# Convolution, token mix and channel mix on one Trainium2 core: five edits to the order of copies, block transfers and last sums

## The chip, the cores and the metric

The kernel runs on one core of one Trainium2 chip. What counts is the device time of one execution in microseconds, and the number given for a kernel is the median of its runs. The kernel before took 2002.95 us (median of 3 runs, 2002.93 to 2003.98). Of one further execution there is a hardware profile: that execution took 2004.08 us, and its span, from the first to the last recorded instruction, is 2002.3 us.

The engines are PE (TensorE, matrix products; PEld is its loading of weights), DVE (VectorE), ACT (ScalarE), POOL (GpSimd) and SP (SyncE, which here only issues transfers). PSUM is the memory into which PE sums, in banks of 512 f32 values per partition.

## The reference

```python
B, S, D = 8, 4096, 192        # batches, tokens, channels; 8 heads of 24 channels, 7 taps
w = softmax(weight)                                        # per head
x = einsum('hk,bskhg->bshg', w, windows(pad_left(x, 6)))   # causal convolution over the tokens
h = relu(x^T @ w_tok1) @ w_tok2                            # token mix, 4096 -> 256 -> 4096
u = x + h^T
out = u + relu(u @ w_ch1) @ w_ch2                          # channel mix, 192 -> 1536 -> 192
```

All is f32. PE gets each f32 operand as two parts, hi (rounded to the type fp32r) and lo (what is left), and a product is made of hi·hi, hi·lo and lo·hi.

## The kernel before, in words

**Groups and tiles.** The batches are worked in five groups: one batch, one batch, and three pairs (`GROUPS = [[0],[1],[2,3],[4,5],[6,7]]`). The tokens of a batch are cut into 8 tiles of 512 tokens. For each tile of a batch the foreground does this, one after the other:

1. Second token product ("mix2", L991/L992 for one batch, L994 to L996 and L1033 for pairs), added on DVE to the convolved input (L1003, L1004): this gives u.
2. u is turned so that channels lie on partitions. In group 0's first tile PE does it (`transposed`, L1059 to L1074). Elsewhere DVE transposes 32x32 blocks (L1006, L1018), and `blocks_sent` (L1099) brings the blocks to their partitions with 16 transfers per call, four steps `k` of four quarters `q`. A quarter with odd `q` goes out on POOL, one with even `q` on SP: 8 and 8.
3. u is split in hi and lo. For a single batch (`parted_single`) that is L1109 on ACT and L1113 on DVE. For a pair (`parted`), three chunks `c`: ACT writes the hi part (L1128, 128x512), DVE the lo part (L1130). Then the halves of the partitions are swapped for the second batch: two copies of all three chunks on ACT, hi first, then lo (L1133, 64x1536 each), and two transfers on POOL the other way (L1135).
4. Product 1 (`channel1`, L1185): six steps of 18 pairs of matmuls over 64 rows, which run on both halves of PE at once. Each step writes a pair of PSUM banks; ACT takes the hi part of relu twice (L1255, `hh`), DVE the lo part once (L1256, `hl`). A step of two sums needs a free pair of banks, so it waits for the L1256 of an earlier step.
5. Product 2 (`channel2`, L1292/L1293, or `channel2_halves`, L1274, in which both halves of PE work again), whose sums DVE adds to u (L1299 and L1303, or L1280 and L1282); then the result is stored (L1322).

PSUM has three pairs of banks for all of this (`ps_x`; `banks()` takes a pair, `bank()` the first bank of one) and two banks for the first token product (`ps_a`).

**Background.** Other work runs between the steps: the convolution of a later group (ACT L725, DVE L727, stored by POOL L762), splitting it (ACT L814, DVE L818), splitting `w_tok1` (ACT L798, DVE L802, POOL L804), the first token product of a later group ("mix1", L830, or L834 to L836 with two batches), and during group 0 also the decoding of `w_tok2` from its bits (ACT L202, L217; DVE L204, L218, L205, L208, L211) and its copying out in another order (`store_t2`: two ACT copies of 128x512, L1423, steps 0 and 1, then a transfer issued by ACT, L1425, step 2).

This is set in order by a planner in the program (`Background`), as the program is written out, not on the chip. Work stands in streams of items. The planner keeps a clock of PE (`pe`) and one of DVE (`dve`), and `fg(pe, dve)` is called at marked places of the foreground with the work of the stretch just written. `fill` then takes items while the DVE clock is less than a margin ahead of PE's: an item is ready if its gate is open and, with a `lag`, if PE's clock has run that far past the end of the item before it in the stream. Of the ready ones the stream that is least done comes first. In product 1 and `channel2_halves` PE works in halves, `bg.tiled` is set, and items that contain PE work are passed over:

```python
if self.tiled and it.pe:
    continue
```

A decoding job has the steps begin, four DVE steps, high (`high(i)`, the ACT copy L217 with lag 0) and low (L218). Jobs for the third and fourth quarter of `w_tok2` wait by their gate until the stores of an earlier quarter are done (`("stored", q2 - 2)`), and the last item of the stream of stores (`through`) opens the memory for the convolution of group 2.

**The end.** The last tokens of the kernel go through `channel2_last`: 12 matmuls hi·(hi, lo) into `both` (L1310), 12 lo·hi into `one` (L1312), the two banks of one pair; then three DVE sums, L1313 from `both`, and L1315 twice, from `both` and from `one`.

Of the kernel before, what the change touches and what calls it, by code (L numbers as in the profile page):

```python
# [22 lines left out]
class Item:  # L23
# [3 lines left out]

    def __init__(self, fn, cost=0.0, lag=0.0, pe=0.0, gate=None, tag=None, eager=False):  # L30
        self.fn, self.cost, self.lag, self.pe, self.gate, self.tag = fn, cost, lag, pe, gate, tag
        self.eager = eager


class Background:
# [52 lines left out]
    def fill(self, until):  # L88
        for s in self.streams:
            while s["items"] and s["items"][0].eager and self.may(s):  # L90
                self.pop(s)
        while True:
            ready = []
            for s in self.streams:
                if s["items"]:
                    it = s["items"][0]
                    at = it.gate() if it.gate else 0.0
                    if self.tiled and it.pe:
                        continue
                    if at is not None and (not it.lag or self.pe >= max(s["free"], at) + it.lag):  # L100
                        ready.append(s)
            if self.dve >= self.pe + until:
                ready = [s for s in ready if s["items"][0].pe]
            if not ready:
                return
            self.pop(min(ready, key=lambda s: s["done"] / s["total"] - s["lead"]))
# [33 lines left out]
def conv_mixer_kernel(ctx: ExitStack, tc: tile.TileContext, x, weight, w_tok1, w_tok2, w_ch1, w_ch2, out):  # L140
# [165 lines left out]
    def decode_items(dec, jobs, loaded=False, pause=None):  # L306
# [26 lines left out]
        def high(i):  # L333
            if not jobs[i][4]:
                return

            def fn():
                jb = sts[i]["jb"]
                hi, lo = jb["make"]() if "make" in jb else (jb["hi"], jb["lo"])
                sts[i]["b"] = dec.b(sts[i], hi, lo, jb.get("view", lambda v: v))  # L340

            add(0, 0, fn, gate=jobs[i][3])

        def low(i):
            def post():
# [737 lines left out]
    def blocks_sent(z, nb, pool, name):  # L1083

        if nb == 1:
            other = own_tile("lo")
            home = other
        else:  # L1090
            other = pool.tile([P, 2, ND, TT], F32R, name=name)
            home = other[:, 1]
        blocks = z[:, :nb * D // QB].rearrange("p (q c) t -> p q (c t)", c=ND)
        home = home.rearrange("p c t -> p (c t)").rearrange("p (i n) -> p i n", i=NQ)
        for k in range(NQ):
            for q in range(NQ):
                i = (q + k) % NQ
                queue = nc.gpsimd if q % 2 else nc.sync
                queue.dma_start(  # L1099
                    out=f32(home[q * QB:(q + 1) * QB, i]),  # L1100
                    in_=blocks[i * QB:(i + 1) * QB, q % (2 * nb)],
                )
        return other
# [16 lines left out]
    def parted(other):  # L1120


        own = own_tile("hi"), own_tile("lo")
        low, high = slice(0, D2), slice(D2, P)
        for c in range(ND):
            v = f32(by_blocks_of(other[:, 1])[:, :, c]).rearrange("p i (j e) -> p j i e", e=QB)
            hi, lo = (o[:, c].rearrange("p (j i e) -> p j i e", i=NQ, e=QB) for o in own)
            nc.scalar.copy(out=hi, in_=v)  # L1128
            bg.fg(0, 700, 0)
            nc.vector.tensor_tensor(out=lo, in0=v, in1=f32(hi), op=ALU.subtract)  # L1130
        swapped = other[:, 0], other[:, 1]
        for k in range(2):
            nc.scalar.copy(out=swapped[k][high], in_=f32(own[k][low]))  # L1133
        for k in range(2):
            nc.gpsimd.dma_start(out=f32(swapped[k][low]), in_=f32(own[k][high]))  # L1135
        own, swapped = (*own, range(ND)), (*swapped, range(ND))
        return [(own, swapped), (swapped, own)]
# [166 lines left out]

    def channel2_last(i, h, u, osb, j):
        ts = slice(j * P, (j + 1) * P)
        pair = banks()
        both, one = pair[:, 0], pair[:, 1]
        for n, f in enumerate(order):
            nc.tensor.matmul(out=both[:, :2 * D], lhsT=h["hh", f][:, ts], rhs=w2[:, f, :], start=n == 0, stop=n == NF - 1)  # L1310
        for n, f in enumerate(order):
            nc.tensor.matmul(out=one[:, :D], lhsT=h["hl", f][:, ts], rhs=w2[:, f, :D], start=n == 0, stop=n == NF - 1)  # L1312
        nc.vector.tensor_tensor(out=rows(osb[:, j]), in0=rows(both[:, :D]), in1=tokens(u, i)[:, j], op=ALU.add)  # L1313
        for v in (both[:, D:2 * D], one[:, :D]):
            nc.vector.tensor_tensor(out=osb[:, j], in0=v, in1=osb[:, j], op=ALU.add)  # L1315
# [51 lines left out]
    def first_items():  # L1367
# [14 lines left out]
        for q2 in range(NS):  # L1382
            for kc in range(KC):
                for r in range(2):
                    a = (q2, kc, r)
                    stores.append(Item(lambda a=a: store_t2(*a, 0), lag=1000, gate=staged(q2)))
                    stores.append(Item(lambda a=a: store_t2(*a, 1), lag=600))
                    stores.append(Item(lambda a=a: store_t2(*a, 2), lag=1200))
            stores.append(Item(lambda q2=q2: stored(q2)))
            for a0 in range(0, ST, TT) if q2 else []:  # L1390
# [187 lines left out]
```

## Time and profile before

| what | value |
|---|---|
| median of 3 runs | 2002.95 us (2002.93 to 2003.98) |
| profiled execution | 2004.08 us |
| its span | 2002.3 us |
| PE busy | 1993.8 us |
| DVE busy | 1465.1 us |
| ACT busy | 763.4 us |
| POOL busy | 229.9 us |

The page gives busy times of each engine, then the span in 40 slices of 50 us, each digit the busy share in tenths. The view of waits lists, for an engine, what it stood still for, in microseconds in all, how often, and the longest. The timeline lists instructions in order of their start, with start and duration in us, the line, the operation, the tiles, a count where equal ones follow one another, and in brackets the idle time before and what ended it. An arrow `a<-b` reads "a from b".

Between the profiled execution and its span lie 1.8 us.

### The profile page before, as it was taken

The numbers are of one execution on the slowest core, as the hardware profiler recorded it, in microseconds if no ns is written. First come the engines' busy times: TensorE is split into PE (matmuls) and PEld (weight loads), VectorE is DVE, ScalarE is ACT, GpSimd is POOL, SyncE is SP. The second block draws the span as 40 slices with busy tenths as digits, with TensorE's granted clock in tenths as the row PEclk, the third lists the DMA queues.
The fourth block names the chain that finished last, engine by engine and source line by source line (L and its number), as shares of the span: only waits on it lengthen the run. The fifth ranks groups of instructions, "written<-read, shape, count | busy, mean of one in ns | idle before, by whom it ended". The sixth has DMA issues, their size and how long they took to land.

```text
span 2002.3 us, 44236 instructions
## 1 busy us (share of the span) xinstructions
PE 1993.8 (100%) x18596; PEld 1846.3 (92%) x18596; DVE 1465.1 (73%) x2474; ACT 763.4 (38%) x1271; POOL 229.9 (11%) x434
## 2 busy tenths in 40 slices
PE   9999999999999999999999999999999999999999
PEld 9898999999999999999989999999999999999998
DVE  8889989999759998744797788446566656665564
ACT  5786433434343343432433433323333322333322
POOL 0001112121211101110011110111111101011110
PEclk9999999999999999999999999999999999999999
DMA  9956456575474456532466434433313233233310
GB/s 308 319 172 211 138 167 198 167 234 173 155 184 131 137 166 196 140 86 53 126 172 203 119 107 140 134 88 85 83 51 78 76 80 81 66 86 85 85 49 17
DMA packets 277046, 267.69 MB, mean 134 GB/s; under 512 B 190928, under 2 KB 224256, under 8 KB 276848
## 3 DMA queue, kind: packets, MB, share of 16 engines
q1 hardware_dynamic: 251744, 182.39, 32.3%
q0 software_dynamic: 22800, 74.08, 12.5%
q10 hardware_dynamic: 2304, 8.39, 1.1%
q8 instruction: 147, 2.41, 0.5%
q14 instruction: 51, 0.42, 0.1%
HBM read 146.31 MB, written 71.30 MB: 109 GB/s over the span
## 4 chain that ended last, share of the span: by engine, by line
PE 93%; DVE 3%; ACT 1%; DMA 1%; issue 1%; SPq 1%; ACTq 0%; DVEq 0%
PE ps_x L1185 38%; PE ps_x L1274 23%; PE ps_x L1292 11%; PE ps_x L1293 5%; PE ps_x L1033 2%; PE ps_a L834 2%; PE ps_a L835 2%; PE ps_a L836 2%; DVE xc L727 1%; PE ps_x L991 1%; PE ps_a L484 1%; PE ps_x L994 1%; PE ps_x L1222 1%; PE ps_a L830 1%; PE ps_x L996 1%; PE ps_x L995 1%
## 5 line engine op out<-in xcount | busy, mean ns | idle before, releaser
L1255 ACT ACTIVATE hh<-ps_x 128x512 fp32r<-128x512 f32 x744 | 404.5, 596 | 843.5 <-PE ps_x L1185 843.3
L1256 DVE SCALAR_TENSOR_TENSOR hl<-ps_x,hh 128x1024 fp32r<-128x1024 f32 x372 | 453.8, 1222 | 228.3 <-ACT hh L1255 227.7
L1274 PE MATMUL ps_x<-w,hh 64*128 64x384 f32 x3360 | 481.6, 355 | 0.0
L1274 PE MATMUL ps_x<-w,hl 64*128 64x192 f32 x3360 | 424.5, 247 | 0.0
L727 DVE SCALAR_TENSOR_TENSOR xc<-raw,cw,xc 128x384 f32<-128x384 f32 (+1 forms) x768 | 385.9, 560 | 7.3 <-ACT xc L725 7.3
L1292 PE MATMUL ps_x<-w,hh 128*128 128x384 f32 x1284 | 370.1, 360 | 0.3 <-DVE hl L1256 0.3
L1185 PE MATMUL ps_x<-other,w_hi 64*128 64x512 f32 x1296 | 336.9, 388 | 0.7 <-ACT other L1133 0.4
L1185 PE MATMUL ps_x<-own_hi,w_hi 64*128 64x512 f32 x1440 | 330.7, 393 | 0.5 <-DVE hl L1256 0.2
L1274 PEld LDWEIGHTS ps_x<-w,hl 64*128 64x128 f32 x3360 | 325.8, 188 | 0.9
L1185 PE MATMUL ps_x<-own_lo,w_hi 64*128 64x512 f32 x1440 | 325.4, 388 | 0.0
L1185 PE MATMUL ps_x<-own_hi,w_lo 64*128 64x512 f32 x1440 | 325.1, 387 | 0.0
L1293 PE MATMUL ps_x<-w,hl 128*128 128x192 f32 x1284 | 321.5, 250 | 0.0
L1274 PEld LDWEIGHTS ps_x<-w,hh 64*128 64x128 f32 x3360 | 319.9, 184 | 0.9
L1185 PEld LDWEIGHTS ps_x<-other,w_hi 64*128 64x128 f32 x1296 | 235.7, 184 | 23.8 <-DVE hl L1256 1.0
L1293 PEld LDWEIGHTS ps_x<-w,hl 128*128 128x128 f32 x1284 | 245.1, 191 | 0.0
L1292 PEld LDWEIGHTS ps_x<-w,hh 128*128 128x128 f32 x1284 | 241.0, 188 | 1.6 <-DVE hl L1256 1.2
L1185 PEld LDWEIGHTS ps_x<-own_lo,w_hi 64*128 64x128 f32 x1440 | 215.4, 184 | 26.0 <-ACT own_lo L1074 0.4
L1185 PEld LDWEIGHTS ps_x<-own_hi,w_lo 64*128 64x128 f32 x1440 | 215.2, 184 | 25.9
L1185 PEld LDWEIGHTS ps_x<-own_hi,w_hi 64*128 64x128 f32 x1440 | 209.5, 184 | 30.9 <-issue 4.1
L1185 PE MATMUL ps_x<-other,w_lo 64*128 64x512 f32 x648 | 181.5, 386 | 0.0
L1282 DVE TENSOR_TENSOR osb<-ps_x,osb 128x192 f32<-128x192 f32 x420 | 150.0, 357 | 14.5
L1280 DVE TENSOR_TENSOR osb<-ps_x,u 128x192 f32<-128x192 f32 x140 | 49.7, 355 | 135.5 <-PE ps_x L1274 135.5
(185 smaller groups left out, 2397.2 us busy)
## 6 DMA issues: line engine op xcount, KB each, us to landing
raw<-in_x_dram SPq DMA_DIRECT2D x56, 672.0 KB, 7.3
t<-t2d SPq DMA_DIRECT2D x64, 512.0 KB, 5.6
u<-xcd SPq DMA_DIRECT2D x62, 384.0 KB, 7.4
xcd<-xc POOLq DMA_DIRECT2D x28, 768.0 KB, 8.4
t<-t1p SPq DMA_DIRECT2D x32, 512.0 KB, 4.3
out_dram<-osb SPq DMA_DIRECT2D x36, 384.0 KB, 3.8
out_dram<-osb POOLq DMA_DIRECT2D x27, 384.0 KB, 3.0
t2d<-stage ACTq DMA_DIRECT2D x16, 512.0 KB, 3.5
```

Source lines behind the costliest of these rows:

```text
L727: nc.vector.scalar_tensor_tensor(out=dst, in0=src, scalar=cw[:, h, k:k + 1], in1=dst, op0=ALU.mult, op1=ALU.add)
L834: nc.tensor.matmul(out=ps, lhsT=wh, rhs=xh, start=a, stop=False)
L835: nc.tensor.matmul(out=ps, lhsT=wh, rhs=xl, start=False, stop=False)
L836: nc.tensor.matmul(out=ps, lhsT=wl, rhs=xh, start=False, stop=z)
L1185: nc.tensor.matmul(out=pss[:, h], lhsT=w1[w][rows, t[h][2][c], p * P:(p + 1) * P], rhs=t[h][v][rows, c], start=a and n == 0, stop=z and n ...
L1255: nc.scalar.activation(out=hh[:, k], in_=pss[:, k], func=AF.Relu)
L1256: nc.vector.scalar_tensor_tensor(out=hl, in0=pss, scalar=0.0, in1=f32(hh), op0=ALU.max, op1=ALU.subtract)
L1274: nc.tensor.matmul(out=ps[:, :m], lhsT=h[part, f][ks, ts], rhs=w2[ks, f, :m], start=n == 0 and part == "hh", stop=z and part == "hl",)
L1280: nc.vector.tensor_tensor(out=rows(osb[:, j]), in0=rows(pss[0][:, :D]), in1=tokens(u, i)[:, j], op=ALU.add)
L1282: nc.vector.tensor_tensor(out=osb[:, j], in0=v, in1=osb[:, j], op=ALU.add)
L1292: nc.tensor.matmul(out=ps[:, :2 * D], lhsT=h["hh", f][:, ts], rhs=w2[:, f, :], start=n == 0, stop=False)
L1293: nc.tensor.matmul(out=ps[:, :D], lhsT=h["hl", f][:, ts], rhs=w2[:, f, :D], start=False, stop=z)
```

## The change

Five edits.

1. An item of the planner can be `long`. While PE works in halves, long items are passed over as those with PE work are. The two ACT copies of `store_t2` are long.
2. The high step of a decoding job has a lag of 300 instead of 0.
3. In `blocks_sent`, the transfer of the last step `k` and the quarter `q` = 0 goes out on POOL. POOL then has 9 of the 16 of a call, SP 7. There are 36 calls.
4. In `parted`, the swapped hi part is copied chunk by chunk in the loop (64x512, right behind the split of that chunk), and the swapped lo part by one copy of 64x1536 after the loop, as before. It is 48 ACT instructions more, two for each of 24 calls.
5. In `channel2_last`, `both` and `one` are the first banks of two pairs, and no longer the two banks of one pair.

```diff
@@ Item
-    def __init__(self, fn, cost=0.0, lag=0.0, pe=0.0, gate=None, tag=None, eager=False):
+    def __init__(self, fn, cost=0.0, lag=0.0, pe=0.0, gate=None, tag=None, eager=False, long=False):
         self.fn, self.cost, self.lag, self.pe, self.gate, self.tag = fn, cost, lag, pe, gate, tag
-        self.eager = eager
+        self.eager, self.long = eager, long
@@ Background.fill
-                    if self.tiled and it.pe:
+                    if self.tiled and (it.pe or it.long):
                         continue
@@ high(i), decoding
-            add(0, 0, fn, gate=jobs[i][3])
+            add(0, 300, fn, gate=jobs[i][3])
@@ blocks_sent
-                queue = nc.gpsimd if q % 2 else nc.sync
+                queue = nc.gpsimd if q % 2 or (k, q) == (NQ - 1, 0) else nc.sync
@@ parted
             nc.vector.tensor_tensor(out=lo, in0=v, in1=f32(hi), op=ALU.subtract)
+            nc.scalar.copy(out=other[high, 0, c], in_=f32(own[0][low, c]))
         swapped = other[:, 0], other[:, 1]
-        for k in range(2):
-            nc.scalar.copy(out=swapped[k][high], in_=f32(own[k][low]))
+        nc.scalar.copy(out=swapped[1][high], in_=f32(own[1][low]))
@@ channel2_last
-        pair = banks()
-        both, one = pair[:, 0], pair[:, 1]
+        both, one = bank(), bank()
@@ first_items
-                    stores.append(Item(lambda a=a: store_t2(*a, 0), lag=1000, gate=staged(q2)))
-                    stores.append(Item(lambda a=a: store_t2(*a, 1), lag=600))
+                    stores.append(Item(lambda a=a: store_t2(*a, 0), lag=1000, gate=staged(q2), long=True))
+                    stores.append(Item(lambda a=a: store_t2(*a, 1), lag=600, long=True))
```

The changed kernel has the same matmuls and the same DVE work. Line numbers are the same up to L1130; the chunk's copy is the new L1131, the lo copy stays L1133, and behind `channel2_last` lines are one less (L1310, L1312, L1313 and L1315 become L1309, L1311, L1312 and L1314; L1423 becomes L1422).

Since the planner places all of the background from its clocks, the edits 1 and 2 move it in groups 0 and 1. Three places follow, each with the program order of one engine.

**Group 0, first tile, DVE up to the first lo part of product 1** (L1256). L278 splits a weight, L1230 adds the sums of the very first tokens, L727 is the convolution, and L204 to L218 decode `w_tok2`. Before:

```order
L278 TENSOR_TENSOR w_1133<-w2f,w_1133 128x4x192 x3
L1230 TENSOR_TENSOR osb<-ps_x,u 128x192
L727 SCALAR_TENSOR_TENSOR xc_926<-raw_751,cw,xc_926 128x8x24 x2
L727 SCALAR_TENSOR_TENSOR xc_926<-raw_754,cw,xc_926 128x8x24 x6
L1230 TENSOR_TENSOR osb<-ps_x,u 128x192
L727 SCALAR_TENSOR_TENSOR xc_926<-raw_754,cw,xc_926 128x8x24 x6
L1256 SCALAR_TENSOR_TENSOR hl_1194<-ps_x,hh_1193 128x1024
```

After:

```order
L278 TENSOR_TENSOR w_1126<-w2f,w_1126 128x4x192 x3
L1230 TENSOR_TENSOR osb<-ps_x,u 128x192
L204 TENSOR_SCALAR dec_top<-dec_top 128x512
L218 TENSOR_TENSOR t2s<-dec_top,t2s 128x512
L205 TENSOR_SCALAR dec_top<-dec_top 128x512
L208 SCALAR_TENSOR_TENSOR dec_top<-dec_raw,dec_top 128x512
L211 SCALAR_TENSOR_TENSOR dec_top<-dec_raw,dec_top 128x512
L727 SCALAR_TENSOR_TENSOR xc_947<-raw_754,cw,xc_947 128x8x24 x2
L1230 TENSOR_TENSOR osb<-ps_x,u 128x192
L727 SCALAR_TENSOR_TENSOR xc_947<-raw_754,cw,xc_947 128x8x24 x6
L1256 SCALAR_TENSOR_TENSOR hl_1186<-ps_x,hh_1185 128x1024
```

Between L278 and the first L1256 stood 14 instructions of the convolution; now 8 of them and a run of five decoding steps stand there. The five stood ahead of these rows before, and six of the convolution have taken their place.

**The boundary from group 1 to group 2, DVE in product 2 of group 1's last tile.** `xc` is group 2's convolved input, L818 makes its lo part for mix1, L802 the lo part of `w_tok1`, L1113 splits u of the last tile, and L1299 and L1303 are product 2's sums of two token blocks each. Before:

```order
L1006 STREAM_TRANSPOSE own_hi<-u 128x3x2x32 x2
L802 TENSOR_TENSOR t_5468<-t_5468 128x2x256
L1299 TENSOR_TENSOR osb<-ps_x,u 128x384
L1303 TENSOR_TENSOR osb<-ps_x,osb 128x384
L818 TENSOR_TENSOR xhl<-xc_5175,xhl 128x768
L1113 TENSOR_TENSOR own_lo<-own_lo,own_hi 128x4x128 x3
L802 TENSOR_TENSOR other<-other 128x2x256
L1299 TENSOR_TENSOR osb<-ps_x,u 128x384
L1303 TENSOR_TENSOR osb<-ps_x,osb 128x384
L818 TENSOR_TENSOR xhl<-xc_5175,xhl 128x768
```

After:

```order
L1006 STREAM_TRANSPOSE own_hi<-u 128x3x2x32 x2
L727 SCALAR_TENSOR_TENSOR xc_5284<-raw_5244,cw,xc_5284 128x16x24 x2
L802 TENSOR_TENSOR t_5558<-t_5558 128x2x256
L727 SCALAR_TENSOR_TENSOR xc_5284<-raw_5244,cw,xc_5284 128x16x24 x4
L1299 TENSOR_TENSOR osb<-ps_x,u 128x384
L1303 TENSOR_TENSOR osb<-ps_x,osb 128x384
L727 SCALAR_TENSOR_TENSOR xc_5284<-raw_5244,cw,xc_5284 128x16x24 x2
L1113 TENSOR_TENSOR own_lo<-own_lo,own_hi 128x4x128 x3
L1299 TENSOR_TENSOR osb<-ps_x,u 128x384
L1303 TENSOR_TENSOR osb<-ps_x,osb 128x384
L818 TENSOR_TENSOR xhl<-xc_5284,xhl 128x768
L802 TENSOR_TENSOR other<-other 128x2x256
```

The end of the convolution came before these rows and now lies among them, and the first L818 stood ahead of L1113 and now stands behind the second L1303. The first matmul of mix1 stands at the same place in PE's order in both.

**Group 2, first tile, ACT in `parted`.** Before:

```order
L1255 ACTIVATE hh_6068<-ps_x 128x512 x4
L1128 CAST own_hi<-other 128x512 x3
L1133 CAST other<-own_hi 64x1536
L1133 CAST other<-own_lo 64x1536
L1255 ACTIVATE hh_6386<-ps_x 128x512 x4
```

After:

```order
L1255 ACTIVATE hh_6068<-ps_x 128x512 x4
L1128 CAST own_hi<-other 128x512
L1131 CAST other<-own_hi 64x512
L1128 CAST own_hi<-other 128x512
L1131 CAST other<-own_hi 64x512
L1128 CAST own_hi<-other 128x512
L1131 CAST other<-own_hi 64x512
L1133 CAST other<-own_lo 64x1536
L1255 ACTIVATE hh_6388<-ps_x 128x512 x4
```

One copy of three chunks became three of one chunk between the splits; the lo copy stayed the last.

## The prediction

> **What bounds the kernel now.** I read the page's head and its chain first, then what PE waited for, then the timeline around each wait.
>
> ```profile
> PE 1993.8 (100%) x18596; PEld 1846.3 (92%) x18596; DVE 1465.1 (73%) x2474; ACT 763.4 (38%) x1271; POOL 229.9 (11%) x434
> ...
> PE 93%; DVE 3%; ACT 1%; DMA 1%; issue 1%; SPq 1%; ACTq 0%; DVEq 0%
> ```
>
> PE is busy for 1993.8 of 2002.3 us. The change removes no matmul, so all that it can touch is what PE stands still, and the ends of the kernel. The view of PE's waits names the places:
>
> ```profile
> PE ps_a L835 <- DVE xhl L818: 0.6, 1, 0.6
> PE ps_x L1185 <- DVE hl L1256: 0.5, 2, 0.3
> ...
> PE ps_x L1185 <- ACT other L1133: 0.4, 1, 0.4
> PE ps_x L1292 <- DVE hl L1256: 0.3, 1, 0.3
> PE ps_x L1185 <- DVE osb L1303: 0.2, 1, 0.2
> ```
>
> Together 2.0 us, each a single place (two for the second row). The brackets count from a modelled end of the matmul before, so the loss is a little larger from start to start; at the two places whose neighbours are quoted below it is 0.7 for a bracket of 0.58 and 0.7 for one of 0.41. By these two I add 0.1 to 0.2 to the other brackets.
>
> **The tail (edit 5).** The last two microseconds, from the timeline:
>
> ```profile
> 1994.87 2.29 PE L1310 MATMUL ps_x<-w,hh 128*128 128x384 f32 x12
> ...
> 1997.00 1.48 PE L1312 MATMUL ps_x<-w,hl 128*128 128x192 f32 x12
> 1998.51 0.36 DVE L1313 TENSOR_TENSOR osb<-ps_x,u 128x192 f32<-128x192 f32 x1 [2.70 <-PE ps_x L1312]
> 1998.90 0.75 DVE L1315 TENSOR_TENSOR osb<-ps_x,osb 128x192 f32<-128x192 f32 x2
> ```
>
> L1313 needs only `both`, finished at 1997.16, but was released by L1312, since the two share a tile. With two tiles, L1313 and the first L1315 run beside the 1.48 us of L1312: two operations of 0.36 and 0.38 against 1.3 us of cover. Behind the last matmul stay one sum instead of three: 0.37 instead of 1998.90 + 0.75 − 1998.51 = 1.14. **−0.8 us**, and PE is at its end there, so nothing takes it back. The second pair is free: of the three, one holds `both`, and of the other two at most one still holds the block before, whose sums are made while L1310 runs. Bounds: −0.8 to 0 (if the last transfer were late for another reason).
>
> **Group 0 (edits 1 and 2).** Three waits lie here. Rows taken out of the timeline, in time order; the L204, L211 and L218 rows give the decoding steps' price.
>
> ```profile
> 123.74 1.40 DVE L727 SCALAR_TENSOR_TENSOR xc<-raw,cw,xc 128x192 f32<-128x192 f32 x4
> 125.05 1.22 DVE L1256 SCALAR_TENSOR_TENSOR hl<-ps_x,hh 128x1024 fp32r<-128x1024 f32 x1
> 125.78 1.15 ACT L1423 CAST stage<-t2s 128x512 fp32r<-128x512 f32 x1
> 126.32 0.96 PE L1185 MATMUL ps_x<-own_hi,w_hi 64*128 64x512 f32 x6 [0.25 <-DVE hl L1256]
> 133.68 0.68 DVE L218 TENSOR_TENSOR t2s<-dec_top,t2s 128x512 fp32r<-128x512 f32 x1
> 135.55 0.44 PE L1292 MATMUL ps_x<-w,hh 128*128 128x384 f32 x1 [0.35 <-DVE hl L1256]
> 136.59 0.69 DVE L211 SCALAR_TENSOR_TENSOR dec_top<-dec_raw,dec_top 128x512 uint32<-128x512 uint32 x1
> 158.77 0.97 PE L1185 MATMUL ps_x<-own_hi,w_hi 64*128 64x512 f32 x6 [0.24 <-DVE osb L1303]
> 160.99 0.42 DVE L204 TENSOR_SCALAR dec_top<-dec_top 128x512 f32<-128x512 f32 x1
> ```
>
> With the copies of 1.15 us out of product 1, ACT's relu is never queued behind one, and the planner hands DVE less background there. But the first wait is DVE's: L1256 at 125.05 started when the convolution ahead of it ended. By the quoted order, DVE now has five decoding steps there (0.42 + 0.68 + 0.42 + 0.69 + 0.69 = 2.9, where L205 and L208 are taken like L204 and L211, of the same size) in place of six convolution steps of 0.35 (2.1). So this L1256 comes 0.8 later and the wait of about 0.4 grows to 1.2: **+0.8**. At 135.55 and 158.77 the decoding and the convolution that DVE had before the sum in question are moved away; I let both go, **−0.8** (0.45 and 0.4). Sum 0, which is an even bet: −1.2 if the run at 125 is done earlier than the order suggests, +1.5 if only the loss comes and one other copy is late. The copies themselves cost nothing where they go: product 2's sums wait for DVE, not ACT, and ACT is busy 38% of the time. The last of them is later in group 0, and with it the convolution of group 2 is opened later; that is the next term.
>
> **The boundary from group 1 to group 2 (edits 1 and 2, late).** Timeline rows around mix1 of group 2:
>
> ```profile
> 538.62 0.95 DVE L818 TENSOR_TENSOR xhl<-xc,xhl 128x768 fp32r<-128x768 f32 x1
> ...
> 542.73 1.90 DVE L1113 TENSOR_TENSOR own_lo<-own_lo,own_hi 128x512 fp32r<-128x512 f32 x3 [3.16 <-ACT own_hi L1109]
> ...
> 544.38 0.34 PE L835 MATMUL ps_a<-xhl,t 128*128 128x384 f32 x1
> 544.54 0.69 DVE L802 TENSOR_TENSOR other<-other 128x512 fp32r<-128x512 f32 x1
> 545.14 0.55 DVE L1299 TENSOR_TENSOR osb<-ps_x,u 128x384 f32<-128x384 f32 x1
> 545.73 0.56 DVE L1303 TENSOR_TENSOR osb<-ps_x,osb 128x384 f32<-128x384 f32 x1
> 546.20 0.95 DVE L818 TENSOR_TENSOR xhl<-xc,xhl 128x768 fp32r<-128x768 f32 x1
> 546.29 0.34 PE L834 MATMUL ps_a<-xhl,other 128*128 128x384 f32 x1
> 547.20 0.44 PE L835 MATMUL ps_a<-xhl,other 128*128 128x384 f32 x1 [0.58 <-DVE xhl L818]
> ```
>
> Each fourth part of mix1 needs one L818. Before, the first was made at 538.62 and the second ended at 547.15, so only the second part stood still: L835 came 0.9 after its L834, where the step is 0.2, a loss of 0.7. In the new order the end of the convolution stands where the first L818 was, and the first L818 stands behind the second L1303. DVE: L1113 ends at 544.63, L1299 and L1303 take till 545.75 (no L802 between), L818 till 546.65. PE is at the first L835 at 544.38, so it loses about 2.25, and the later parts follow at DVE's 0.95 + 0.69 = 1.65 for each against PE's 1.9 (546.29 − 544.38), without further loss. **+1.55** (2.25 − 0.7). The eight convolution steps that now stand ahead are hidden in the 3.16 us in which DVE idled for L1109, and in the like stretch before the first L1299. Bounds: 0 if DVE is early enough that L1113 is done before; +2.2 if the blocks for L1109 land 0.6 late (below).
>
> **The swap in `parted` (edit 4).** ACT rows of group 2's first tile, PE's first pairs, the price of one 64x512 copy, and another call:
>
> ```profile
> 638.27 1.66 ACT L1128 CAST own_hi<-other 128x512 fp32r<-128x512 f32 x3 [13.45 <-DMA other<-own_hi]
> 639.97 1.48 ACT L1133 CAST other<-own_hi 64x1536 fp32r<-64x1536 f32 x1
> 640.59 0.50 PE L1185 MATMUL ps_x<-own_hi,w_hi 64*128 64x512 f32 x1
> 641.50 0.50 PE L1185 MATMUL ps_x<-other,w_hi 64*128 64x512 f32 x1 [0.41 <-ACT other L1133]
> 643.01 0.39 PE L1185 MATMUL ps_x<-other,w_hi 64*128 64x512 f32 x1
> ...
> 1067.08 1.66 ACT L1128 CAST own_hi<-other 128x512 fp32r<-128x512 f32 x3 [12.21 <-DMA other<-own_hi]
> 1072.14 0.39 PE L1185 MATMUL ps_x<-other,w_hi 64*128 64x512 f32 x1
> ...
> L1074 ACT CAST own_lo<-own_lo 64x512 fp32r<-64x512 f32 x4 | 2.5, 620 | 0.1
> ```
>
> Before, all of hi is there at 641.45 and lo at 642.82. Now each chunk costs a split and a copy that needs it, 0.62 each by the L1074 row: chunks at 639.5, 640.75, 642.0, and lo (1.48 more) at 643.5. PE would be ready at 640.59, 0.23 a pair: the first two chunks are in time, the third is needed at 641.05 and comes 0.9 late, and lo, needed at 643.01 − 0.68 = 642.3, is 1.15 late in all. Before the loss was 0.7. So the total delay of the step is **+0.45**: the copy is chunked, but the chain behind it, 5.2 us instead of 4.55, ends later. The same margin rule at other calls: at 1067.08 lo is there at 1072.3 against 1072.14, 0.2 late; one call at 1010 is like it. The others of the 24 start their split over a microsecond earlier against PE. **+0.8** in all; 0 if the copies flow behind one another at 0.5 (the L1133 row's 1.48 for three) without waiting for the split's end, +1.6 if the wait costs another 0.15 per chunk. The waiting copy holds ACT, and behind it DVE's L1130 of the next chunk, about 1.2 us longer in each call; DVE has convolution behind that, and POOL's transfers for the second batch have the whole of product 1 to land.
>
> **Nine on POOL, seven on SP (edit 3).** The issues, and one POOL issue that waited:
>
> ```profile
> L1099 SPq DMA_DIRECT2D other<-own_hi x104: 512/588/1597, 572.9 to 1318.3; - x104
> L1099 POOL DMA_DIRECT2D other<-own_hi x104: 498/498/536, 573.3 to 1318.0; - x104
> ...
> 537.58 0.50 POOL L1099 DMA_DIRECT2D own_lo<-own_hi  x1 [0.95 <-DMA own_lo<-own_hi]
> ```
>
> Eight issues take SP 8 × 0.59 = 4.7 and POOL 8 × 0.50 = 4.0, and POOL starts 0.4 to 0.5 later; with 7 and 9 SP ends at 4.1 and POOL at 4.9 to 5.0. So the last issue ends 0.2 later, not earlier. The last row shows a POOL issue held until an earlier POOL transfer had landed; a ninth meets that more often. I take **0**, since L1109 or L1128 is mostly well ahead of PE; bounds −0.3 and +1 (0.2 at each tight place above, and 0.6 at the boundary).
>
> The rows show POOL's issue at 0.50 in nearly every case, so DVE does not hold it up there. The Trainium skill (SBUF — State Buffer, section "A bandwidth-pool intuition that's wrong" and the box before it) warns that a transfer issued by GpSimd can starve while VectorE runs a two-port operation, and advises SyncE or ScalarE; that speaks against this edit. By it each ninth transfer would wait for the DVE operation in flight, at most an L1256 of 1.22 us; the maximum of 0.54 us among 104 speaks against it, and it is priced in the third rival.
>
> **Sum.** −0.8 + 0 + 1.55 + 0.8 + 0 = +1.55. Against the profiled execution (2004.08; 1.8 us lie around its span) that is 2005.6; that execution lies 1.1 above the median of the runs, and against the median of 2002.95 it is **2004.5**. Its own bounds, taking half of each term's spread together: 2002.5 to 2006.5. A change of 0.2% (4.0 us) is about what a measurement can tell from none: 1998.95 to 2006.95 is no change.
>
> **The rivals.**
>
> 1. *The waits go and none comes.* The five waits of the view (0.7 + 0.4 + 0.45 + 0.4 + 0.7, start to start) and the tail, 0.8: −3.4, to 1999.5. For it: the edits aim at each. Against it: the quoted orders put the first L818 and the first L1256 later, not earlier.
> 2. *Slower: DVE is late at the boundary.* The eight convolution steps put there take some 4.5 us (0.56 each, as L1299's size), and have the 3.16 us idle stretch and the one before the first L1299. If ACT's part of the convolution, which follows the later opening of group 2's work, makes them end over 3 us later than room allows, every further microsecond stands before L1113, L1299 and L818, and PE waits it out in full. From 2.5 us beyond that room it exceeds the bound: +1.55 + 3.5 = +5, to 2008. For it: the convolution is behind through all of group 1. Against it: DVE idled at this place, and PE's other needs come first in DVE's order.
> 3. *The ninth POOL transfer.* It waits for the first's landing, about 0.5 more at each of the three tight places and the boundary: +2 on top, to 2006.5. For it the row at 537.58; against it that it is one POOL row of 0.95 in all.
> 4. *Nothing moves but the tail.* The waits change places and sizes and add to nothing: 2002.2.
>
> **How the numbers follow.** Chances: forecast 0.58, first rival 0.14, second 0.12, third 0.06, fourth 0.10. The range leaves out most of the second rival and the lower part of the first: 1999.6 to 2006.8. Faster by over 0.2% needs more than all the waits named: 0.03. Slower by over 0.2%: the second rival and the upper end of the third, 0.13. The same: 0.84.
>
> **What would show it.** In the changed profile: L1314 once behind the last matmul, 0.4 us (tail); PE's wait for L818 at the first L835 of group 2's mix1, about 2 us; one at the first product 1, about 1 us, for L1256; none for L1303 in group 0; at about 641 a wait for L1131 or L1133 of 0.5 to 1. The forecast is wrong if PE's row for L818 is gone or below 0.6, or above 4; the term for `parted` if the copies stand 0.5 apart and no wait for L1133's lo part shows.

## The result, and the profile after

The changed kernel takes **2022.77 us** (median of 5 runs, 2018.92 to 2024.03); the kernel before 2002.95 (5 runs, 2002.8 to 2003.98). The ratio is 1.0092, interval 1.0081 to 1.0104: slower by 19.8 us between the medians, by 16 to 21 by the interval, above the upper end of the stated range (2006.8) and above the time of every rival. The profiled execution took 2018.92 us, its span is 2016.7. It is the fastest of the five, so the places found in it add up to some 14 us and not to 19.8. Of its 14.4 us more than the span before, 7.0 are time in which PE stood still, and 7.4 are longer busy time (2001.2 against 1993.8), largely where matmuls came one by one or at about half the clock.

The head of the page and the chain:

```profile
span 2016.7 us, 44225 instructions
...
PE 2001.2 (99%) x18596; PEld 1846.9 (92%) x18596; DVE 1468.9 (73%) x2474; ACT 776.8 (39%) x1319; POOL 246.1 (12%) x470
...
PE 88%; DVE 6%; ACT 2%; DMA 1%; issue 1%; POOL 1%; SPq 0%; ACTq 0%; DVEq 0%; POOLq 0%
```

The work is the same (DVE 1465.1 before, ACT 13 us more for 48 instructions more), but the chain now runs 6% through DVE and 2% through ACT (3% and 1% before). PE's waits:

```profile
PE ps_x L1185 <- DVE hl L1256: 2.1, 2, 1.3
PE ps_x L1185 <- ACT own_hi L1128: 1.7, 3, 1.4
PE ps_a L835 <- DVE xhl L818: 1.6, 1, 1.6
PE ps_a L834 <- ACT xhl L814: 1.6, 1, 1.6
...
PE ps_x L1185 <- ACT other L1133: 1.2, 3, 0.4
PE ps_x L1185 <- ACT other L1131: 0.6, 4, 0.2
```

Apart from L1131, the copy that the change put in, two of these lines are new: PE waits for L1128, the split of blocks that have just arrived, and for L814, which stands on ACT behind such a split. Matching PE's matmuls one by one with those before, the loss sits in few places: 2.1 us at 291 to 295, 2.9 at 548 to 550, 0.8 at 646, 5.8 at 952 to 972, and 1.4 each at 1028 and 1086; the tail gives back 0.5.

**The largest place** is the call of block transfers at 952. In the kernel before the same call stands at 945. SP, then POOL:

```profile
945.74 4.96 SPq L1099 DMA_DIRECT2D other<-own_hi  x8
950.74 6.20 SPq L715 DMA_DIRECT2D raw<-in_x_dram  x4
```

```profile
946.27 3.94 POOL L1099 DMA_DIRECT2D other<-own_hi  x8 [21.05 <-DVE own_hi L1018]
```

SP, then POOL, from the timeline of the changed kernel:

```profile
951.81 4.32 SPq L1099 DMA_DIRECT2D other<-own_hi  x7
956.18 7.48 SPq L715 DMA_DIRECT2D raw<-in_x_dram  x4
```

```profile
952.34 1.98 POOL L1099 DMA_DIRECT2D other<-own_hi  x4 [21.06 <-DVE own_hi L1018]
956.44 2.44 POOL L1099 DMA_DIRECT2D other<-own_hi  x5 [2.12 <-issue]
```

and what waited for them on ACT, with PE's clock (the last number but two) in the windows behind it:

```profile
963.98 0.62 ACT L1128 CAST own_hi<-other 128x512 fp32r<-128x512 f32 x1 [21.75 <-DMA raw<-in_x_dram]
```

```profile
964.00:968.00 4.00, 2.60 (x7) 1.04 (x9) 2.18 (x4) 3.75 (x7) 0.52 (x1) 1.00 1.06 293
968.00:970.00 2.00, 2.00 (x10) 1.24 (x12) 0.93 (x2) 1.40 (x1) 1.43 (x3) 0.58 0.83 183
970.00:972.00 2.00, 2.00 (x14) 1.54 (x12) 0.00 (x0) 0.86 (x2) 1.20 (x3) 0.57 0.99 234
```

POOL stopped for 2.12 us after four of its nine, for no reason that the profile shows. Meanwhile SP, through with its seven, issued the raw loads of the next convolution (L715, 672 KB each), which in the kernel before follow all sixteen blocks. POOL's last five blocks (48 KB each), issued 956.4 to 958.4, landed at 959.8 to 963.7 by the trace's landings, 3.4 to 5.6 us after their issue; 2.0 is the median of the trace. PE stood for 1.4 us, then took each chunk as it came (seven matmuls in the 4 us from 964), and its granted clock was 0.58 and 0.57 for the next 4 us, in which it was busy throughout: another 2 × 0.42 + 2 × 0.43 = 1.7 us.

**The boundary from group 1 to group 2:**

```profile
546.34 1.90 DVE L1113 TENSOR_TENSOR own_lo<-own_lo,own_hi 128x512 fp32r<-128x512 f32 x3 [4.21 <-ACT own_hi L1109]
548.13 0.44 PE L834 MATMUL ps_a<-xhl,t 128*128 128x384 f32 x1 [1.60 <-ACT xhl L814]
548.15 0.55 DVE L1299 TENSOR_TENSOR osb<-ps_x,u 128x384 f32<-128x384 f32 x1
549.21 0.95 DVE L818 TENSOR_TENSOR xhl<-xc,xhl 128x768 fp32r<-128x768 f32 x1
550.21 0.44 PE L835 MATMUL ps_a<-xhl,t 128*128 128x384 f32 x1 [1.65 <-DVE xhl L818]
```

The first L835 waits for the first L818 behind L1299 and L1303, as the quoted order had it. But L1113 starts 3.6 us later than before, against 2.2 us of delay up to there, since the blocks for L1109 came late (POOL stopped for 2.73 us in that call as well), and L814, behind L1109 on ACT, holds PE's first L834. No raw load is near this call, and POOL's last five blocks landed 1.7 to 1.8 us after their issue: here the stop alone made them late.

**The end of group 0,** where the prediction had no term:

```profile
287.64 1.12 ACT L725 ACTIVATE xc<-raw,cw 128x384 f32<-128x384 f32 x2 [5.88 <-POOL raw L717]
...
292.00 2.20 DVE L727 SCALAR_TENSOR_TENSOR xc<-raw,cw,xc 128x384 f32<-128x384 f32 x4
294.12 2.35 DVE L1256 SCALAR_TENSOR_TENSOR hl<-ps_x,hh 128x1024 fp32r<-128x1024 f32 x2
...
295.39 0.96 PE L1185 MATMUL ps_x<-own_hi,w_hi 64*128 64x512 f32 x6 [1.32 <-DVE hl L1256]
```

Convolution that had ended before this place now stands between PE's banks and the L1256 that frees them.

**The tail** did what was expected. From the end of the last matmul to the end of the last sum it is 0.40 us, where it was 1.18; the profiled execution keeps 0.5 of the 0.8, since its end follows the last sum 0.26 later than before:

```profile
2011.91 1.48 PE L1311 MATMUL ps_x<-w,hl 128*128 128x192 f32 x12
2012.11 0.36 DVE L1312 TENSOR_TENSOR osb<-ps_x,u 128x192 f32<-128x192 f32 x1 [1.38 <-PE ps_x L1309]
2012.51 0.36 DVE L1314 TENSOR_TENSOR osb<-ps_x,osb 128x192 f32<-128x192 f32 x1
2013.43 0.36 DVE L1314 TENSOR_TENSOR osb<-ps_x,osb 128x192 f32<-128x192 f32 x1 [0.57 <-PE ps_x L1311]
```

### The profile page after: what moved, and what is told of

Read it like the earlier page. It is cut to its first block, busy times and chain, and to the rows that moved or that the text cites. A ratio compares the mean times of both kernels' runs of the same rounds, so it can differ in the third digit from the quotient of the medians.

```text
span 2016.7 us, 44225 instructions
## 1 busy us (share of the span) xinstructions
PE 2001.2 (99%) x18596; PEld 1846.9 (92%) x18596; DVE 1468.9 (73%) x2474; ACT 776.8 (39%) x1319; POOL 246.1 (12%) x470
## 4 chain that ended last, share of the span: by engine, by line
PE 88%; DVE 6%; ACT 2%; DMA 1%; issue 1%; POOL 1%; SPq 0%; ACTq 0%; DVEq 0%; POOLq 0%
PE ps_x L1185 37%; PE ps_x L1274 23%; PE ps_x L1292 10%; PE ps_x L1293 4%; PE ps_x L1033 2%; DVE xc L727 2%; PE ps_a L834 2%; PE ps_a L835 2%; PE ps_a L836 2%; DVE hl L1256 1%; PE ps_a L484 1%; PE ps_x L1222 1%; PE ps_x L994 1%; DMA raw<-in_x_dram 1%; PE ps_a L830 1%
## 5 line engine op out<-in xcount | busy, mean ns | idle before, releaser
L1256 DVE SCALAR_TENSOR_TENSOR hl<-ps_x,hh 128x1024 fp32r<-128x1024 f32 x372 | 453.8, 1223 | 216.8 <-ACT hh L1255 216.1
L727 DVE SCALAR_TENSOR_TENSOR xc<-raw,cw,xc 128x384 f32<-128x384 f32 (+1 forms) x768 | 385.3, 561 | 9.1 <-ACT xc L725 9.1
L1274 PEld LDWEIGHTS ps_x<-w,hl 64*128 64x128 f32 x3360 | 331.2, 188 | 0.8
L1274 PEld LDWEIGHTS ps_x<-w,hh 64*128 64x128 f32 x3360 | 325.4, 184 | 0.8
```

Source lines behind the costliest of these rows:

```text
L727: nc.vector.scalar_tensor_tensor(out=dst, in0=src, scalar=cw[:, h, k:k + 1], in1=dst, op0=ALU.mult, op1=ALU.add)
L1256: nc.vector.scalar_tensor_tensor(out=hl, in0=pss, scalar=0.0, in1=f32(hh), op0=ALU.max, op1=ALU.subtract)
L1274: nc.tensor.matmul(out=ps[:, :m], lhsT=h[part, f][ks, ts], rhs=w2[ks, f, :m], start=n == 0 and part == "hh", stop=z and part == "hl",)
```

## The experiments

The time beside each is the median; the kernel before, on the same chip in the same hour, took 2003.3 to 2003.8.

### The edits one at a time

Each is the kernel before with its part of the change alone. The diffs here and below show the lines that matter and leave out the rest; a word behind # names the version.

```diff
+                queue = nc.gpsimd if q % 2 or (k, q) == (NQ - 1, 0) else nc.sync   # nine
```

> The kernel before with edit 3 alone (POOL issues nine of sixteen). Theory A (POOL): in the changed kernel's trace POOL stops for 2.7 us at 538.8 and 2.1 us at 954.3 in the middle of a call, without a releaser, the rest of the blocks lands behind the raw loads that SP issues next (963.7 instead of about 957.5), and PE loses some 5.6 us there and some of the 4.6 us at 548. Then this kernel alone is slower by 4 to 9 us, 2007 to 2012, with such a stop inside a call. Theory B (edits 1 and 2 carry it, the order of the background): nine on POOL is harmless, 2002.5 to 2004. Theory C (the chunked copies carry it): the same as B.

**2011.68** against 2003.33, ratio 1.0043 (1.0026 to 1.0060): +8.4, theory A's size. At the end of its trace PE is 6.6 us behind the kernel before, and 6.5 of them are lost in one call, at 944. SP, POOL, and what PE waited for:

```profile
944.31 4.33 SPq L1099 DMA_DIRECT2D other<-own_hi  x7
948.68 7.54 SPq L715 DMA_DIRECT2D raw<-in_x_dram  x4
```

```profile
944.84 0.51 POOL L1099 DMA_DIRECT2D other<-own_hi  x1 [21.05 <-DVE own_hi L1018]
947.62 3.90 POOL L1099 DMA_DIRECT2D other<-own_hi  x8 [2.27 <-issue]
```

```profile
957.49 0.50 PE L1185 MATMUL ps_x<-own_hi,w_hi 64*128 64x512 f32 x1 [1.76 <-ACT own_hi L1128]
960.04 0.79 PE L1185 MATMUL ps_x<-other,w_hi 64*128 64x512 f32 x1 [2.04 <-ACT other L1133]
```

POOL stopped for 2.27 us behind its first block, so five of its nine went out behind SP's first load and landed 4.0 to 5.9 us after their issue; behind the 3.8 us of waits the clock was 0.50 from 960 to 964. In eight other calls only POOL's last block went out behind a load. It landed after 2.3 to 5.2 us, and PE lost by it in one of them, 1.0 us at 1077.

```diff
+            nc.scalar.copy(out=other[high, 0, c], in_=f32(own[0][low, c]))             # chunks
```

> The kernel before with edit 4 alone (swapped hi copied chunk by chunk). Theory C: in the changed kernel each chunk takes 1.30 us on ACT, the chain 5.44 us instead of 4.55, and PE loses 0.8, 1.4 and 1.4 us at three tight calls (641, 1010 and 1067 in the kernel before): about +3.5, 2006 to 2007. Theory A, in which these calls only lose because the blocks landed late: +0.5 to +1, 2003.5 to 2004. Theory B: the same as A.

**2006.27** against 2003.33, 1.0014 (1.0005 to 1.0023): +2.9, theory C. The copies as the changed kernel's timeline shows them:

```profile
643.28 0.62 ACT L1128 CAST own_hi<-other 128x512 fp32r<-128x512 f32 x1 [13.39 <-DMA other<-own_hi]
643.93 0.62 ACT L1131 CAST other<-own_hi 64x512 fp32r<-64x512 f32 x1
644.57 0.62 ACT L1128 CAST own_hi<-other 128x512 fp32r<-128x512 f32 x1
...
647.24 1.48 ACT L1133 CAST other<-own_lo 64x1536 fp32r<-64x1536 f32 x1
```

Each split and each copy begins only when the one before has ended, 0.65 us apart, where three splits alone took 0.55 each: the lo copy ends 5.44 us after the start instead of 4.55. In the trace of edit 4 alone, which is the fastest of its ten runs, the three calls that theory C names lose 0.7, 0.8 and 0.6 us.

```diff
+                    if self.tiled and (it.pe or it.long):                               # long
+            add(0, 300, fn, gate=jobs[i][3])                                            # lag
```

> The kernel before with edits 1 and 2 alone (long copies out of product 1, lag 300). Theory B: the convolution comes late at the ends of groups 0 and 1; PE loses 1.9 us at 291 to 295 and about 2 us at the first L835 of group 2's mix1 (0.7 before), while the waits at 135 and 158 go: +3 to +5, 2006 to 2008. Theory A: the loss at 548 is mostly the blocks' (L1109 at 545.7 instead of 542.1), so without edit 3 it is +1 to +2.5, 2004 to 2005.5.

**2017.26** against 2003.33, 1.0068 (1.0053 to 1.0083): +13.9, above both theories. The boundaries are as theory B has them (a loss of 1.7 at 300 and 1.9 at the first L835), but there is also a stop of POOL of 2.0 us in the call at 1013, with eight on POOL and eight on SP. POOL's last block went out behind the loads and landed after 5.1 us, PE waited 3.6 us for the split and the copies behind it, and with the low clock behind the waits this call loses 5.6 us. So it does not take a ninth transfer to make blocks late.

> The kernel before with edit 5 alone (two pairs of banks in the last sums). All theories: nothing but the tail moves, one DVE sum behind the last matmul instead of three: -0.8 us, 2002.1 to 2002.3. Rival: the output transfer behind it sets the end and the gain is under 0.3.

**2002.49** against 2003.33, 0.9995 (0.9985 to 1.0004): the size is the expected one, and the interval includes no change.

> Edit 1 alone (long copies of store_t2 kept out of product 1, the decoding's lag left at 0). If edit 1 makes the convolution late: waits of some 1.5 us for L1256 at about 295 and of 2 us for L818 at the first L835 of group 2's mix1 (0.7 before) as with edits 1 and 2 together, +3 to +5 without a stop of POOL inside a call, and +8 to +14 with one. If the lag did it: within 1.5 of 2003.3 without such a stop.

**2007.29** against 2003.54, 1.0021 (1.0011 to 1.0030): +3.8, nearly all of it one wait for L1303 at 161 (3.1 us from start to start); the boundaries are as before (0.7 for L818).

> Edit 2 alone (the lag of 300 in the decoding). Edit 1 alone gave +3.8 (one wait of 3.1 us at 161, the boundaries as before), both gave +14. If the waits at 126 (0.9), 295 (1.5) and 552 (1.9 for L818) are the lag's, they are here too: +3 to +5 without a stop of POOL in a tight call, +8 to +11 with one. If they come only from both together: within 1.5 of 2003.4.

**2005.30** against 2003.76, 1.0007 (0.9998 to 1.0016): the interval includes no change, and the boundaries stay as before here too, with a wait of 0.9 at 126 and 1.3 at 158. The late convolution at the ends of groups 0 and 1 comes only from both edits together. All five taken apart (8.4 + 2.9 + 13.9 − 0.8) make 24.4, more than the 19.8 of the whole: edit 3 alone and edits 1 and 2 alone each have one call in which POOL stops and loads pass its blocks (6.5 and 5.6 us in their traces), and the changed kernel has one such call too (5.8), not two.

### What makes the blocks late: three theories that fell

First I took POOL's stop for the cause and looked for what it goes by: by count of POOL's instructions (A2), by rows moved (R), by count of transfers (S).

```diff
+    pad = const.tile([P, 8], F32, name="pad")
+    for _ in range(18):                       # 8 in the others
+        nc.gpsimd.memset(pad, 0.0)
```

> The kernel before with 18 POOL memsets of 128x8 added ahead of the group loop, nothing else. Theory A2 (the stop is POOL's own, by count of its instructions, and not made by nine transfers): in the traces POOL stops for 2 to 3 us at about its 251st to 263rd, 438th to 451st and 648th record. In the kernel before, the second of these falls into idle time; 18 more instructions move it into the call of group 2's last tile (945 to 950), so this kernel stops there, the blocks land behind the raw loads, PE stands 3 to 5 us and the granted clock falls to about 0.5 for some 4 us behind: +5 to +8, 2008 to 2011. Rival (the stop comes from a ninth transfer or from a full queue): nothing, within 1 of 2003.3.

> The changed kernel with 8 POOL memsets added ahead of the group loop. Theory A2: the stops at records 263 and 441 leave the calls at 537 and 952 for the idle stretches ahead of them: the loss of 5.6 us and the lower clock at 964 go and the one at 548 shrinks by 1 to 1.5: 6 to 9 us faster than the changed kernel, 2013 to 2016. Rival (nine transfers make the stop): as the changed kernel, 2019 to 2024.

> Edit 3 alone, with the same 8 memsets. Theory A2: the stop at record 438 (in the call at 944.8 with edit 3 alone, 2011.7) moves into idle time, and what is left is edit 3's own price: 2003 to 2005. Rival (nine transfers themselves are late): 2010 to 2013.

**2021.22, 2041.90 and 2030.45**: A2 fell. The stops stand at the same transfers as without memsets (in the kernel before, the stop ahead of the store of L762 at 532 stands ahead of the same store, at 533). The kernels are slower for another reason, all through the span from group 2 on. PE's matmuls of product 1 in the kernel before and, behind it, with 18 memsets:

```profile
L1185 PE MATMUL ps_x<-other,w_lo 64*128 64x512 f32 x648 | 181.5, 386 | 0.0
```

```profile
L1185 PE MATMUL ps_x<-other,w_lo 64*128 64x512 f32 x648 | 185.4, 392 | 0.0
```

The new tile takes 32 bytes of each partition ahead of most others; that their shift slows these matmuls by 6 ns each (3 to 4 ns from start to start) was not tested by itself.

```diff
+    scratch = dram.tile([P, H], F32, name="scratch")
+    for _ in range(2):
+        nc.gpsimd.dma_start(out=scratch, in_=csm)
```

> The kernel before with two small POOL transfers added ahead of the group loop (128 rows each, to a scratch in DRAM that nobody reads). Theory R: POOL stops for 2 to 3 us each time its transfers have used up some 13.5 thousand rows (in seven traces at 13,024 to 13,952, 27,232 to 27,360 and 40,352 to 40,384 rows); 18 memsets moved the stop's record number by 18, not its transfer. In the kernel before the second stop lies just behind the call at 1003 (27,136 to 27,392 rows), hidden in idle time; 256 rows more move it into that call: the last blocks land 4 to 6 us later behind the raw loads, PE stands 3 to 4 us and the granted clock falls behind it: +4 to +7, 2007 to 2011. Rival (the stop goes by something else): within 1 of 2003.4.

> The changed kernel with the same two transfers. Theory R: the stops at 13,024 and 27,328 rows move 256 rows back, out of the calls at 537 and 952 into idle time: the 5.6 us and the low clock at 964 go, and 1 to 1.5 us at 548: 5 to 8 us faster than the changed kernel (2022.8), 2014 to 2018. Rival (nine transfers or the new order make POOL late): 2019 to 2025.

> Edit 3 alone, with the same two transfers. Theory R: the stop at 27,232 rows in the call at 944.8 moves ahead of the call into idle time; what is left is edit 3's own price: 2003 to 2006 (2011.7 with the stop). Rival: 2010 to 2013.

> Edits 1 and 2 alone, with the same two transfers. Theory R: the stop at 27,360 rows in the call at 1014 moves ahead of it; PE's 3.9 us there and the low clock behind go, and what is left is the order of the background (the waits at 129, 260, 300 and 552 in that trace, together about +5): 2008 to 2012 (2017.3 with the stop). Rival (the order makes those blocks late as well): 2016 to 2018.

**2003.32, 2023.59, 2010.98 and 2016.56**: R fell in all four; the stops are still in the same calls, and no time moved by more than a microsecond.

```diff
+                queue = nc.gpsimd if q % 2 or (k == NQ - 1 and q % 2 == 0) else nc.sync      # ten
+                queue = nc.gpsimd if q % 2 and (k, q) != (NQ - 1, 1) else nc.sync            # seven
```

> The kernel before with ten of the sixteen on POOL and six on SP. Theory S (the stop comes after a set count of POOL's transfers, the second 95 behind the first): with ten in each call the 95 end in the call at 887 or ahead of it, whose blocks have some 4 us to spare, and no stop falls into the calls at 945 and 1003: 2003 to 2007, faster than nine (2011.7). Rival N (each transfer moved to POOL is late in itself): worse than nine, 2013 to 2020, with the same waits for L1128 at about 957.

> The kernel before with seven of the sixteen on POOL and nine on SP. Theory S: the 95 transfers end in the call at 1003 (the sixth of its seven), which is one of the tight ones: PE waits 2 to 4 us for L1128 at about 1013 and the granted clock falls behind it: 2006 to 2010. Rival N (POOL's transfers are the late ones): nothing or a little faster, 2002 to 2004.

> The changed kernel with ten of the sixteen on POOL instead of nine. Theory S: the second stop leaves the call at 952; the 5.6 us at 964 and the low clock go: 5 to 8 us faster than the changed kernel, 2014 to 2018. Rival N: 2023 to 2030.

Ten: **2028.93** against 2003.76, 1.0126 (1.0109 to 1.0143), and **2040.91** in the changed kernel. Seven: **2005.23**, 1.0008 (0.9998 to 1.0017). Both times with ten lie above the ranges of both theories, and seven lies between the two. S fell: with seven there is no stop in the call at 1003, and with ten there is none in any of the tight calls (those whose blocks PE needs almost at once), and yet all of them lose (five calls, 3.5 to 4.9 us each in the trace). SP's and POOL's rows of one such call with ten, and what waited:

```profile
634.84 3.69 SPq L1099 DMA_DIRECT2D other<-own_hi  x6
638.65 1.57 SPq L715 DMA_DIRECT2D raw<-in_x_dram  x2
```

```profile
636.58 3.91 POOL L1099 DMA_DIRECT2D other<-own_hi  x8 [0.18 <-issue]
```

```profile
645.88 1.66 ACT L1128 CAST own_hi<-other 128x512 fp32r<-128x512 f32 x3 [16.33 <-DMA other<-own_hi]
649.10 0.70 PE L1185 MATMUL ps_x<-other,w_hi 64*128 64x512 f32 x1 [2.04 <-ACT other L1133]
```

POOL's issues run through to 640.5, but its last four, from 638.5 on, land at 642.2 to 645.4: 3.6 to 5.4 us after their issue, where the six before them took 1.8 to 2.3; SP's first raw load was issued at 638.65. With nine alone the same holds for one transfer: in the call at 754, POOL's ninth, issued 758.91, 0.13 us behind SP's first raw load, landed 5.2 us later, all others in 1.8 to 2.2.

### Theory Q: the raw loads

```diff
+        if nb == 2:
+            nc.sync.dma_start(out=scratch, in_=f32(home[QB:2 * QB, 0, 0:8]))
```

This goes behind the loops of `blocks_sent`: 32 rows of 32 bytes that SP may read only when POOL's third last transfer (of ten) or second last (of nine) has landed. The transfers on POOL stay as they were. I call this small transfer the guard. Lines move by 2 to 4.

> Ten of sixteen on POOL (2028.9 alone), and in each call for a pair one small SP transfer behind SP's six, which reads what POOL's third last transfer writes; so SP issues its raw loads only when that has landed. Theory Q (POOL's last transfers queue behind the raw loads that SP issues as soon as its shorter share is out): the landings come back to about 2 us after the issue, the waits of 2 to 4 us for L1128 and L1133 at 587, 646, 970, 1029 and 1092 go, and so does the low clock: 2003 to 2009. Rival (POOL's transfers are slower or later in themselves): 2025 to 2032.

**2006.77** against 2003.32, 1.0014 (1.0005 to 1.0024), instead of 2028.93: 22 of the 25 us are gone. The same call as above, SP and ACT:

```profile
633.39 3.70 SPq L1101 DMA_DIRECT2D other<-own_hi  x6
640.66 0.32 SPq L1106 DMA_DIRECT2D scratch<-other  x1
641.09 1.26 SPq L715 DMA_DIRECT2D raw<-in_x_dram  x2
```

```profile
641.45 1.66 ACT L1132 CAST own_hi<-other 128x512 fp32r<-128x512 f32 x3 [13.35 <-DMA other<-own_hi]
```

The split starts 8.1 us after SP's first block, where it was 11.0 (645.88 − 634.84). POOL's last four blocks land 2.5 to 3.4 us after their issue in this call, and 1.7 to 2.3 us in the calls at 949, 1006 and 1063. What is left in this trace, some 3 us, is lost in groups 0 and 1, whose calls have no guard.

> The changed kernel with the same guard. Theory Q: the 5.6 us and the low clock at 964 go, also where POOL's own stop of 2 us falls into that call; left are the order of the background (about 2.4 us at 291 to 295 and 2.9 at 548) and the longer chain of copies (0.8 + 1.4 + 1.4): 7 to 10 us faster than the changed kernel, 2012 to 2016. Rival: 2021 to 2025.

**2016.77** against 2003.32, 1.0065 (1.0050 to 1.0080), 6.0 us less than the changed kernel; that is a microsecond less than expected. In its trace the call at 956, in which POOL stops as before, loses 1.7 us instead of 5.8. SP, then POOL:

```profile
955.84 4.33 SPq L1101 DMA_DIRECT2D other<-own_hi  x7
963.75 0.33 SPq L1106 DMA_DIRECT2D scratch<-other  x1
964.12 6.21 SPq L715 DMA_DIRECT2D raw<-in_x_dram  x4
```

```profile
960.47 2.45 POOL L1101 DMA_DIRECT2D other<-own_hi  x5 [2.13 <-issue]
```

These five landed 1.7 to 2.1 us after their issue. The 13.8 us by which this trace is behind the kernel before lie at the end of group 0 (3.8), at the boundary to group 2 (4.5: the guard is not on the calls of single batches, so L814 still holds L834 for 1.7) and at the calls of `parted` (some 5).

No version measured is faster than the kernel before by more than the measurement is uncertain; edit 5 alone comes nearest.

## Why the prediction was wrong

- **Nine on POOL (0 predicted, +8.4 measured alone; the third rival had +2).** This step failed. It compared when the last issue ends, 0.2 us later, and stopped there. What SP issues next was named nowhere: raw loads of 672 KB. With eight and eight SP's blocks end last (950.70 against 950.21 in the call at 945 of the kernel before), and the loads stand behind all blocks. With seven SP is done first, and what POOL has still to send stands behind a load: up to 5.2 us to land instead of 2. Holding back the loads and nothing else gave back 22 of 25 us with ten on POOL, and in the changed kernel 4 us in the call where POOL stops. With nine alone, though, one late block seldom cost PE anything: 6.5 us are lost in the single call in which POOL also stopped, and five blocks were late. The prediction had no term for such a stop. In all seven traces with nine on POOL one lies in that same call, and in the kernel before it does not; no run shows why, and nine without the stop was not run, so how the 8.4 us divide between loads and stop stays open. The rule of the Trainium skill that was weighed (SBUF — State Buffer, section "A bandwidth-pool intuition that's wrong" and the box before it, on VectorE starving GpSimd) spoke against the edit for a reason that no run here shows: POOL's issues of blocks stayed at 0.50 us (at most 0.53 in the changed kernel).
- **Group 0 (0 predicted; +2.1 in the profile, at the end of the group).** The wait at 126 grew to 0.9 of the predicted 1.2 and those at 135 and 158 went, so that sum was right. It missed the end of the group: late convolution ahead of what PE waits for, the second rival's mechanism, was there with 2.1 us, one boundary earlier than the rival looked for it.
- **The boundary to group 2 (+1.55 predicted; +2.9 in the profile).** The order held: L835 lost 1.9 of the predicted 2.25, 1.2 more than before. The term itself left out that the blocks for L1109 would be late, which only its upper bound allowed for (0.6 us); a stop of POOL made them so, and that added the 1.7 at L834.
- **Chunked copies (+0.8 predicted; +2.9 measured alone).** The mechanism was right and the size was off: the chain is 5.44 us, not 5.2, and three calls lost 0.8, 1.4 and 1.4 in the changed kernel, and 0.7, 0.8 and 0.6 in the trace of edit 4 alone, where the sum had 0.45, 0.2 and about 0.2. In the changed kernel the blocks also came later.
- **The tail (−0.8 predicted).** Right: one sum of 0.36 us stays behind the last matmul. Alone it measured −0.8, a size that the measurement cannot tell from none, but its trace shows the 0.8 at the place.
- **Waits were counted at their length.** After the long ones PE's granted clock was 0.50 to 0.58 for about 4 us, 1.7 us of loss in the changed kernel, which the sum had nowhere.

## What to carry to other kernels

Before moving a transfer from one queue to another, look at what the relieved queue issues next: it comes earlier by as much, and small transfers that something waits for then stand behind it. A chain of copies cut into pieces is ready sooner at its head and later at its end, so ask which piece the reader needs last. And a planner's table is one system: two edits that left both boundaries as they were when made alone moved them together.

## What the runs showed of the hardware

- A 48 KB transfer issued by POOL 0.1 to 2.4 us behind a 672 KB load of SP landed after 3.3 to 6.0 us instead of 2, in the traces of the changed kernel and of nine and ten alone; the five issued within 0.1 us of a load took 2.2 to 3.3. The Trainium skill (DMA: Bandwidth & Descriptors, section on queues, rings and completion order) says that each transfer engine takes turns between the queues that have work, a packet at a time; by that the small transfer shares with the load and does not pass it, and the landings here fit that, though no run shows the turns themselves.
- After PE had stood or crept for some 4 us, its granted clock was low for a while: 0.58 and 0.57 over 4 us in the changed kernel, 0.50 and 0.67 over 4 us with edits 1 and 2 alone, 0.81, 0.50 and 0.84 over the 6 us from 648 with ten alone, and 0.50 at 960 to 964 within a longer stretch with nine alone. Counted as time at half clock the first three are 3.3 to 3.4 us each (for the first, 2 × 0.42 + 2 × 0.43, divided by 0.5). The Trainium skill (TensorE: Matmul & The Clock Gate, Part 1) gives an idle window of about 3.4 us that halves the clock and a busy one that restores it; the length of the low stretches agrees, but PE need not be idle: in the changed kernel it did seven matmuls, 2.6 us of busy time, in the 4 us before.
- POOL stops for 2.0 to 2.9 us without a releaser, at few places in each kernel. Neither memsets nor small transfers moved it predictably, and what it goes by stays open. Where loads passed what POOL had still to send, the call lost 5.6 to 6.5 us. Where none did, late blocks could still cost 1.7 us: at L834 of the changed kernel, and in the call at 956 of the changed kernel with the guard.
